# Loading q and k in 1 KB runs of four tokens, with a new order of work around the transposes, in a fused attention and feed-forward kernel

## The chip, the cores and the metric

The kernel runs on one core of a Trainium2 chip. The metric is the device time of one execution in microseconds (us), and lower is better. A run of one program was repeated several times. The engines are PE (matrix multiplications and transposes), VectorE (DVE in the profile), ScalarE (ACT), GpSimd (POOL) and SyncE (SP), which here only issues DMA transfers.

## The reference

The reference computes forgetting attention (causal attention with a decay per token) for 8 batches, 8 heads, 576 tokens and a head size of 64. The result goes straight into a feed-forward block with SiLU.

```python
scores = (q @ k.transpose(0, 1, 3, 2)) / sqrt(D)              # [8, 8, 576, 576]
cum    = cumsum(log(clip(f, 1e-4, 1)), axis=-1)
scores = where(causal, -1e9, scores + cum[..., :, None] - cum[..., None, :])
attn   = softmax(scores)                                      # max, exp, divide by the sum
x      = (attn @ v) -> tokens x (heads * D)                   # [4608, 512]
h      = x @ w_in                                             # [4608, 2048]
out    = (h * sigmoid(h)) @ w_out                             # [4608, 512]
```

q and k are random numbers times 0.1, so the scaled scores are small, and the weights of the attention come mostly from the decay.

## The kernel before

The attention is worked off in 32 pairs of heads (8 batches of 4 pairs). The loop runs once for each pair, `n` from 0 to 31. q and k must be transposed so that the head size lies on the partitions. PE does this by a matrix multiplication with the identity, into PSUM, and VectorE copies the result to SBUF as `qkT`. The scores are then made in three chunks, ScalarE takes the exponential, and VectorE masks the diagonal blocks. For each two pairs PE also makes the denominators (`den`), VectorE takes their reciprocal, and eight DMA transfers spread it over partitions (`rb`). The numerators (`num`) are multiplied by `rb` into `xT`, the input of the feed-forward block.

`fill(n)` puts n pieces of feed-forward work (each four matmuls of 512 columns) between these steps, so that PE has something to do while it waits for the others. There is none before the first 512 tokens of `xT` are complete, which needs a whole batch. So there is a *head*, in which attention runs alone, and a *steady part*, in which PE is nearly always busy.

Each engine works off its instructions in the order in which the program gives them: in the trace of the kernel before, a copy on VectorE whose input was ready at about 228.5 us starts at 231.25, behind a reciprocal of 3.75 us that stands before it in the program. Scores, transposes, denominators and numerators share two PSUM buffers (`psc`).

```python
    psc = ctx.enter_context(tc.tile_pool(name="psc", bufs=2, space=bass.MemoryType.PSUM))
    # ... (cut)
    def load_qk(b, c, h0, h1):                      # issued by GpSimd, converts to bf16
        # ... (cut)
        for i, src in enumerate((q, k)):
            nc.gpsimd.dma_start(
                out=qkb[b][:n, i, c, h0 * D : h1 * D].rearrange("p (h d) -> p h d", d=D),
                in_=src[b, h0:h1, c * P : c * P + n, :].rearrange("h p d -> p h d"),
            )
    # ... (cut)
    def transposes(n):
        # ... (cut)
        tp = psc.tile([P, 2, 1024], BF16, name="tp", tag="sc")
        for i in range(2):                          # q, k
            for c in range(NM + 1):                 # four blocks of 128 tokens, one of 64
                nk = P if c < NM else ST
                nc.tensor.transpose(
                    tp[:, i, c * P : c * P + nk],
                    src[:nk, i, c, p * P : (p + 1) * P],
                    ident_bf[:nk, :nk],
                )
        t = qktp.tile([P, 2, S], BF16, name="qkT", tag="qkT")
        nc.vector.tensor_copy(out=t[:, :, :], in_=tp[:, :, 0:S])      # one copy of 1152 columns
        qkT[n] = t
    # ... (cut)
    def den(qd):                                    # for the pairs 2*qd and 2*qd+1
        # ... 36 small matmuls into dn (cut)
        rec = recp.tile([P, S], FP32, name="rec", tag="rec")
        nc.vector.reciprocal(out=rec[:, :], in_=dn[:, 0:S])
        # ... eight nc.sync.dma_start: rb <- rec (cut)
    # ... (cut)
    for hh in range(2):
        for c in range(NM + 1):
            convert_v(0, c, hh * H // 2, (hh + 1) * H // 2, nc.vector)   # v times its decay
    transposes(0)
    for n in range(NU):
        b, p = divmod(n, NP)
        scores(n, 0)
        fill(1)
        # ... loads of the next batch; convert_v of the next batch on GpSimd (cut)
        scores(n, 1)
        fill(1)
        scores(n, 2)
        fill(2)
        if n % 2 == 0 and n >= 2:
            den(n // 2 - 1)
            fill(2)
        if n % 2 == 1 and n >= 3:
            num(n - 3)
            fill(1)
            num(n - 2)
            fill(1)
            finished(n - 2)
        if n + 1 < NU:
            transposes(n + 1)
        fill(2)
```

The softmax here doesn't subtract the row's maximum and nothing guards it: scores larger than these inputs give would overflow.

## Time and profile before

The time before was 456.11 us (median of 3 runs, 455.33 to 456.65).

The profile is of one execution. Its page gives the busy time of each engine first. Then it divides the span into 40 slices of 11.4 us, and each digit is the busy share in tenths (9 is 90% or more). These are lines of the page of the kernel before:

```profile
span 454.3 us, 7436 instructions
PE 381.1 (84%) x2966; PEld 175.3 (39%) x3013; DVE 232.7 (51%) x337; ACT 202.4 (45%) x312; POOL 118.5 (26%) x154
...
PE   0155236989998999899989998999899989999996
...
DMA  9999999996359635953597309830203021300011
...
DMA packets 128561, 42.57 MB, mean 94 GB/s; under 512 B 115664, under 2 KB 119760, under 8 KB 128528
```

PE is nearly full from the eighth slice on (80 us), and half empty before it. The DMA engines are busy 90% or more in the first nine slices. Most packets are short: one token of one head is 256 bytes.

The view of groups of instructions shows a line of the program, engine, operation, output and input with their sizes, then "busy us, mean ns of one", then the idle time before these instructions and what ended it. The copy of q and k and the two larger masks, before:

```profile
L202 DVE COPY qkT<-tp 128x1152 bf16<-128x1152 bf16 x32 | 23.7, 740 | 16.4 <-PE tp L196 16.4
L253 DVE TENSOR_TENSOR u<-u,mask 128x768 bf16<-128x768 bf16 x32 | 18.4, 575 | 67.8 <-ACT u L240 67.7
L257 DVE TENSOR_TENSOR u<-u,mask 128x256 bf16<-128x256 bf16 x32 | 9.1, 284 | 0.0
```

The view of waits says for which releaser an engine stood still: us in total, number of times, longest. For PE between 167.3 and 303.8 us (three periods of four pairs), before, the largest is:

```profile
PE sc L233 <- DVE qkT L202: 6.9, 6, 1.7
```

The scores wait for the copy of q and k every second pair. The timeline shows why. Its columns are the start and the duration in us, the engine, the line, the operation, and in brackets how long the engine had been idle and what released it. Before, in the steady part:

```profile
226.44 3.75 DVE L293 RECIPROCAL rec<-dn 128x576 f32<-128x576 f32 x1
...
227.55 0.98 PE L196 MATMUL tp<-ident_bf,qkb 128*128 128x128 bf16 x10
...
231.25 0.75 DVE L202 COPY qkT<-tp 128x1152 bf16<-128x1152 bf16 x1
...
232.06 0.39 PE L233 MATMUL sc<-qkT 64*128 64x512 bf16 x2 [1.70 <-DVE qkT L202]
```

The transposes are done soon after 228.5, but their copy stands behind the 3.75 us reciprocal in VectorE's queue. In the head there is another wait, much longer. These are lines of the timeline of the kernel before, around 48 to 62 us:

```profile
48.52 11.05 SPq L299 DMA_DIRECT2D rb<-rec  x8
...
60.86 0.76 DVE L326 TENSOR_TENSOR xT<-nm,rb 128x576 bf16<-128x576 f32 x1 [13.81 <-DMA rb<-rec]
...
61.67 1.46 PE L196 MATMUL tp<-ident_bf,qkb 128*128 128x128 bf16 x10 [13.10 <-DVE xT L326]
```

The reciprocal had ended at 42.0 us. Its broadcasts stood behind the loads of v in the queue of SyncE and were issued from 48.5 to 59.6. PE had no buffer in the meantime.

### The profile page before, as it was taken

What the parts mean: (1) busy time and instruction counts of PE and PEld (TensorE: products, weight loads), DVE (VectorE), ACT (ScalarE), POOL (GpSimd) and SP (SyncE); (2) the same over time, 40 slices, a digit from 0 to 9 for tenths busy, and PEclk for the clock granted to TensorE, in tenths of its full rate; (3) what the DMA queues carried; (4) which work ended last, traced back from release to release, by engine and by line L of the source; (5) the groups of instructions that cost most, each with busy time, mean ns of one, the idle gap of its engine ahead of it and who ended that gap; (6) DMA issues with size and microseconds to landing.
All of it is one profiled execution on the core that took longest, in us unless ns stands there. A gap on an engine that the chain in (4) does not pass through costs nothing.

```text
span 454.3 us, 7436 instructions
## 1 busy us (share of the span) xinstructions
PE 381.1 (84%) x2966; PEld 175.3 (39%) x3013; DVE 232.7 (51%) x337; ACT 202.4 (45%) x312; POOL 118.5 (26%) x154
## 2 busy tenths in 40 slices
PE   0155236989998999899989998999899989999996
PEld 0133113434443444344434443444344434444442
DVE  2335026684468446835683558455845585274310
ACT  3054022564366436643664356435643562264421
POOL 9843943470047004700470047000000000000000
PEclk9999999999999999999999999999999999999999
DMA  9999999996359635953597309830203021300011
GB/s 158 103 180 157 194 184 169 177 115 67 95 133 120 60 100 127 124 57 100 128 116 65 100 25 107 73 100 26 52 25 91 34 52 38 108 1 24 26 68 69
DMA packets 128561, 42.57 MB, mean 94 GB/s; under 512 B 115664, under 2 KB 119760, under 8 KB 128528
## 3 DMA queue, kind: packets, MB, share of 16 engines
q0 software_dynamic: 79392, 13.64, 41.1%
q1 hardware_dynamic: 49136, 28.47, 25.7%
q8 instruction: 23, 0.38, 0.4%
q14 instruction: 10, 0.08, 0.1%
HBM read 36.85 MB, written 9.44 MB: 102 GB/s over the span
## 4 chain that ended last, share of the span: by engine, by line
PE 48%; DMA 13%; issue 12%; DVE 11%; ACT 7%; SPq 4%; POOL 4%; DVEq 0%; POOLq 0%; ACTq 0%
PE po L371 27%; PE hp L344 10%; DMA rb<-rec 8%; ACT u L240 6%; DVE gt L353 5%; PE nm L314 4%; DMA qkb<-in_q_dram 4%; SPq L299 4%; PE sc L233 3%; DVE rec L293 3%; POOL qkb L70 3%; PE tp L196 3%; PE dn L285 1%; DMA qkb<-in_k_dram 1%; ACT th L352 1%
## 5 line engine op out<-in xcount | busy, mean ns | idle before, releaser
L240 ACT ACTIVATE u<-sc 128x1024 bf16<-128x1024 f32 x96 | 97.5, 1028 | 93.9 <-PE sc L233 69.2
L344 PE MATMUL hp<-xT,w_in_bf 128*128 128x512 bf16 x551 | 136.8, 380 | 2.9 <-issue 1.1
L371 PE MATMUL po<-w_out_bf,gt 128*128 128x512 bf16 x554 | 134.3, 380 | 2.6 <-issue 2.1
L353 DVE SCALAR_TENSOR_TENSOR gt<-th,hp 128x512 bf16<-128x512 bf16 x144 | 95.9, 683 | 52.2 <-ACT th L352 52.2
L352 ACT ACTIVATE th<-hp 128x512 bf16<-128x512 f32 x144 | 86.8, 605 | 77.0 <-PE hp L344 70.5
L371 PEld LDWEIGHTS <-gt 128*128 128x128 bf16 x576 | 50.8, 98 | 59.0 <-issue 5.2
L344 PEld LDWEIGHTS <-w_in_bf 128*128 128x128 bf16 x576 | 49.9, 98 | 58.9 <-issue 7.5
L233 PE MATMUL sc<-qkT 64*128 64x512 bf16 (+4 forms) x320 | 40.6, 325 | 31.9 <-DVE qkT L202 26.9
L293 DVE RECIPROCAL rec<-dn 128x576 f32<-128x576 f32 x16 | 60.1, 3755 | 6.3 <-PE dn L285 6.3
L380 ACT ACTIVATE osb<-po 128x512 f32<-128x512 f32 x36 | 21.5, 597 | 73.5 <-PE po L371 46.6
L253 DVE TENSOR_TENSOR u<-u,mask 128x768 bf16<-128x768 bf16 x32 | 18.4, 575 | 67.8 <-ACT u L240 67.7
L70 POOL DMA_DIRECT2D qkb<-in_q_dram x45 | 38.8, 861 | 39.1 <-PE tp L196 34.0
L326 DVE TENSOR_TENSOR xT<-nm,rb 128x576 bf16<-128x576 f32 x32 | 24.2, 756 | 45.0 <-DMA rb<-rec 23.9
L196 PE MATMUL tp<-ident_bf,qkb 128*128 128x128 bf16 (+1 forms) x320 | 34.5, 231 | 13.3 <-DVE xT L326 13.1
L70 POOL DMA_DIRECT2D qkb<-in_k_dram x45 | 38.2, 849 | 11.2 <-DMA w_in_bf<-in_moe_w_in_dram 4.8
L233 PEld LDWEIGHTS <-qkT 64*128 64x128 bf16 x320 | 11.7, 98 | 70.8 <-DVE qkT L202 36.6
L196 PEld LDWEIGHTS <-qkb 128*128 128x128 bf16 (+1 forms) x320 | 24.3, 102 | 28.8 <-issue 15.4
L202 DVE COPY qkT<-tp 128x1152 bf16<-128x1152 bf16 x32 | 23.7, 740 | 16.4 <-PE tp L196 16.4
L314 PE MATMUL nm<-u,vp 128*64 128x64 bf16 (+4 forms) x512 | 30.0, 264 | 0.2
L314 PEld LDWEIGHTS <-vp 128*64 128x64 bf16 x512 | 20.1, 117 | 17.9 <-issue 12.7
L155 PE MATMUL wps<-ident_f,wexp 64*128 64x64 f32 x5 | 0.8, 322 | 17.8 <-POOL ident_f masks.py:199 17.8
L285 PEld LDWEIGHTS <-w_bf 128*32 128x32 bf16 (+1 forms) x576 | 10.9, 100 | 10.8 <-issue 6.4
(73 smaller groups left out, 121.0 us busy)
## 6 DMA issues: line engine op xcount, KB each, us to landing
rb<-rec SPq DMA_DIRECT2D x128, 72.0 KB, 2.1
out_dram<-osb SPq DMA_DIRECT2D x36, 256.0 KB, 2.0
qkb<-in_q_dram POOLq DMA_DIRECT2D x28, 128.0 KB, 6.8
qkb<-in_k_dram POOLq DMA_DIRECT2D x28, 128.0 KB, 7.0
w_in_bf<-in_moe_w_in_dram POOLq DMA_DIRECT2D x4, 512.0 KB, 10.0
w_out_bf<-in_moe_w_out_dram POOLq DMA_DIRECT2D x4, 512.0 KB, 11.4
qkb<-in_q_dram POOLq DMA_DIRECT2D x15, 64.0 KB, 5.9
qkb<-in_k_dram POOLq DMA_DIRECT2D x15, 64.0 KB, 5.8
```

The costliest lines, as they stand in the source:

```text
L70: nc.gpsimd.dma_start(out=qkb[b][:n, i, c, h0 * D : h1 * D].rearrange("p (h d) -> p h d", d=D), in_=src[b, h0:h1, c * P : c * P + n, :].re ...
L196: nc.tensor.transpose(tp[:, i, c * P : c * P + nk], src[:nk, i, c, p * P : (p + 1) * P], ident_bf[:nk, :nk],)
L202: nc.vector.tensor_copy(out=t[:, :, :], in_=tp[:, :, 0:S])
L233: nc.tensor.matmul(sc[:, i, col : col + q1 - q0], lhsT=t[r, 1, kb * P : (kb + 1) * P], rhs=t[r, 0, q0:q1], start=True, stop=True,)
L240: nc.scalar.activation(out=u[:, :, c * 512 : (c + 1) * 512], in_=sc[:, :, :], func=ACT.Exp, scale=scale)
L293: nc.vector.reciprocal(out=rec[:, :], in_=dn[:, 0:S])
L314: nc.tensor.matmul(nm[i * D : (i + 1) * D, q0:q1], lhsT=v_t[r, p, :] if kb == NM else vp[:, kb, 2 * p + i, :], rhs=(ut[r, :] if kb == NM e ...
L326: nc.vector.tensor_tensor(out=xT[:, p, b * S : (b + 1) * S], in0=nm[:, 0:S], in1=rb[:, :], op=ALU.mult)
L344: nc.tensor.matmul(hp[:, :], lhsT=w_in_bf[:, cc, fc * P : (fc + 1) * P], rhs=xT[:, cc, t0 : t0 + TG], start=(cc == 0), stop=(cc == NCC - 1),)
L352: nc.scalar.activation(out=th[:, :], in_=hp[:, :], func=ACT.Tanh, scale=0.5)
L353: nc.vector.scalar_tensor_tensor(out=gt[:, fc, :], in0=th[:, :], scalar=1.0, in1=hp[:, :], op0=ALU.add, op1=ALU.mult,)
L371: nc.tensor.matmul(po[:, :], lhsT=gt[:, fc, tb * P : (tb + 1) * P], rhs=w_out_bf[:, fc, :], start=(fc == 0), stop=(fc == NFC - 1),)
```

## The change

The intent: shorten the head, and free the copy of q and k from the reciprocal.

1. *Loads.* q and k are loaded by SyncE as fp32, one pair at a time, with four tokens in a row on one partition. One piece is then 4 x 256 bytes = 1 KB instead of 256 bytes. GpSimd converts them to bf16. The last 64 tokens of a batch are loaded apart.
2. *Order of tokens.* Partition p now holds the tokens 4p to 4p+3. After the transposes the columns in PSUM are in the order (j, p) instead of (p, j), so VectorE reorders when it copies. One copy becomes three.
3. *Order of work.* The transposes of the next pair come ahead of the denominators. The reciprocal is done in two halves, with fill work between. The numerators of two pairs come one iteration earlier.
4. *Along with it.* v of batch 0 is now multiplied by its decay on GpSimd, not on VectorE before the first pair. It stands in the program at the third pair, but GpSimd runs ahead and comes to it sooner (at 17.46 us in the trace after, where the third pair starts at 35.4). The weights are loaded later (`w_in` at n = 2, `w_out` at n = 6).

The diff, cut to its core:

```diff
-    def load_qk(b, c, h0, h1):
+    def load_qk(n):
+        b, p = divmod(n, NP)
         ...
+            nc.sync.dma_start(
+                out=t[:, :, :],
+                in_=src[b, 2 * p : 2 * p + 2, 0:SM, :].rearrange("h (p j) d -> p h (j d)", j=NJ),
+            )
         ...  (load_tails, cast_qk, cast_tails: cut)
     def transposes(n):
         ...
+            for j in range(NJ):
                 nc.tensor.transpose(
+                    tp[:, i, j * P : (j + 1) * P], src[:, i, j, :], ident_bf[:, :]
                 )
         ...
-        nc.vector.tensor_copy(out=t[:, :, :], in_=tp[:, :, 0:S])
+        for i in range(2):
+            nc.vector.tensor_copy(
+                out=t[:, i, 0:SM].rearrange("r (p j) -> r j p", j=NJ),
+                in_=tp[:, i, 0:SM].rearrange("r (j p) -> r j p", j=NJ),
+            )
+        nc.vector.tensor_copy(out=t[:, :, SM:S], in_=tp[:, :, SM:S])
         ...
+    def rec_part(qd, part):
+        dn, rec = dens[qd]
+        r = slice(part * S // 2, (part + 1) * S // 2)
+        nc.vector.reciprocal(out=rec[:, r], in_=dn[:, r])
         ...
     for n in range(NU):
         b, p = divmod(n, NP)
         scores(n, 0)
         fill(1)
+        if n + 1 < NU:
+            last_cast = cast_qk(n + 1, (nc.gpsimd, nc.gpsimd))
+        if n + 4 < NU:
+            load_qk(n + 4)
+        if n == 2:
+            with tc.issue_after(last_cast.ins):
+                for c in range(NM + 1):
+                    convert_v(0, c, 0, H, nc.gpsimd)
+                for i in range(WQ):
+                    load_w_in(i)
+        if n == 6:
+            with tc.issue_after(last_cast.ins):
+                for i in range(WQ):
+                    load_w_out(i)
         ...
         scores(n, 2)
         fill(2)
-        if n % 2 == 0 and n >= 2:
-            den(n // 2 - 1)
-            fill(2)
-        if n % 2 == 1 and n >= 3:
-            num(n - 3)
+        if n + 1 < NU:
+            transposes(n + 1)
+        fill(1)
+        if n % 2 == 1:
             fill(1)
+            den(n // 2)
+            rec_part(n // 2, 0)
+            fill(1)
+            rec_part(n // 2, 1)
+            fill(1)
+        elif n >= 2:
             num(n - 2)
             fill(1)
-            finished(n - 2)
-        if n + 1 < NU:
-            transposes(n + 1)
-        fill(2)
-    den(NU // 2 - 1)
+            num(n - 1)
+            fill(2)
+            finished(n - 1)
```

## The prediction

> **What bounds the kernel now.** Two regimes. From 80 us on, the tensor engine (PE) binds: in the windows view it is busy 94 to 95% (37.3 of 40 us at 160-200, 95.3 of 100 at 300-400), and in the chain of waits the same place of the loop returns every 45.1 to 46.1 us per four head pairs, 11.4 us a pair. Before 80 us PE works only about 30 us. The first feed-forward matmul of a ready group comes near 81 us.
>
> The head's causes, in the timeline: GpSimd issues 20 q/k loads of 0.75 to 0.85 us each until 16.7 us, and only then builds the identities, so the first transposes start at 18.5 and the first scores at 24.0. The DMA engines are saturated (page: nine tenths for the first 8 slices; 115664 of 128561 packets under 512 B). The copy of the next q/k stands behind the 3.76 us reciprocal (PE idle 3.1 us at 39.5). The reciprocal's broadcast DMAs stand behind value loads on the sync queue: they are issued from 48.5 to 59.6 although the reciprocal ended at 42.0, and PE is idle from 48.6 to 61.7.
>
> **Removed.** The q/k loads on GpSimd (77 us of its queue). About 73,700 short q/k packets become some 24,600, of which 16,400 are 1 KB[...]. Head: scores start at about 12 us (estimate: decay weights ready at 8.0 as now, transposes 0.8 + 1.5, copies 1.5), not 24. Transposes ahead of the denominators free the copy from the reciprocal: in steady state that wait costs PE 1.7 + 0.9 us per four pairs. Numerators of a pair of pairs come one iteration earlier, so group 0 is ready at the start of n=5, not at the end.
>
> **Added.** Copy out of PSUM: one of 740 ns becomes three. [...] +24 us of VectorE in all (51% to some 60%), off the path in steady state, about +0.7 us a pair in the head. GpSimd gets casts of perhaps 0.6 to 1 us each (estimate from its 1.04 us for a 128x512 multiply), 2 a pair: hidden. More loads go through the sync queue, so broadcasts may still wait. PE work itself doesn't change.
>
> **Sum.** Estimated head: pairs 0 and 1 at 5.7 us, 2 to 4 at 8 to 11 us because reciprocal and broadcast still hold the two PSUM buffers. Iteration 5 starts, with feed-forward work to fill in, at about 55 us. Before, iteration 6 starts near 83.5; one pair of 11.4 us apart, so the head gains about 17 us. 27 iterations at 11.1 us (were 11.35; floor 10.8) give 300, the end (one leftover run of fills, numerators, 64 chunks at 0.865, last store) about 70: 55 + 300 + 70 = 425. Predicted 426 us, range 413 to 442; faster by over 2%: 0.92, within 2%: 0.05, slower: 0.03.
>
> **What would show it.** Right: timeline with scores by 13 us, feed-forward by 60; PE in the windows at 0-80 up from 30 to about 50 us; q/k copies near 1.5 us per pair; under 85,000 packets; the steady waits of scores for the copy gone; period of four pairs at 44 to 45 us. Wrong: period over 45.5 us, with PE waiting for VectorE (gt, rec) instead.
>
> **What would make it wrong.** Broadcasts stuck behind q/k and value loads on the one sync queue; weights, now issued only after pair 3's casts, arriving after 55 us; denominators, now right behind their own scores, waiting for masks; GpSimd casts slowing VectorE.

With the other go the three terms of the copies, which came to 1.5 us a pair. The rest counts with it: +24 us of VectorE is 32 x (1.5 - 0.74), and the +0.7 us a pair in the head is the same difference. The sum came to 55 + 300 + 70 = 425 us, put down as 426.

## The result, and the profile after

The time after was 448.81 us (median of 4 runs, 448.28 to 450.13). The ratio is 0.984, with a 95% interval of 0.981 to 0.987: 1.6% faster. That is clear of the noise, but under 2%. Ratios in this document are the mean time of one kernel's fast runs over that of the kernel before's fast runs of the same rounds. They are not quite the ratios of the medians quoted. The prediction, 426 us, asked for four times that gain, and the measured time lies outside its range.

The same lines of the page after (slices of 11.2 us):

```profile
span 448.4 us, 7690 instructions
PE 390.3 (87%) x3013; PEld 177.7 (40%) x3013; DVE 290.5 (65%) x406; ACT 204.7 (46%) x312; POOL 97.5 (22%) x149
...
PE   2236676899979999999989998999899989999996
...
DMA  8995959975666365425642423250203020400011
...
DMA packets 79156, 52.03 MB, mean 116 GB/s; under 512 B 49872, under 2 KB 70352, under 8 KB 79120
```

The loads did what was asked of them. There are 79,156 packets instead of 128,561, and PE works earlier. VectorE is the surprise: 290.5 us busy instead of 232.7. The groups after show from where:

```profile
L243 DVE COPY qkT<-tp 128x512 bf16<-128x512 bf16 x64 | 79.2, 1322 | 27.4 <-PE tp L238 27.4
L247 DVE COPY qkT<-tp 128x128 bf16<-128x128 bf16 x32 | 8.1, 252 | 0.0
L298 DVE TENSOR_TENSOR u<-u,mask 128x768 bf16<-128x768 bf16 x32 | 22.2, 692 | 32.1 <-ACT u L285 32.1
L302 DVE TENSOR_TENSOR u<-u,mask 128x256 bf16<-128x256 bf16 x32 | 12.9, 402 | 0.0
```

The copies of one pair take 1.32 + 1.32 + 0.25 = 2.9 us, where one took 0.74. The prediction had 1.5. The masks, which nobody touched, are longer on average as well: 692 instead of 575 ns and 402 instead of 284 ns.

The waits of PE in the same window (167.3 to 303.8 us), after:

```profile
PE hp L396 <- DVE gt L405: 3.0, 3, 1.0
PE sc L278 <- ACT u L285: 1.8, 6, 0.3
```

The wait of the scores for the copy has gone, as intended. In its place PE waits for the SiLU product `gt` on VectorE. The timeline after shows how that comes about:

```profile
217.27 2.45 DVE L243 COPY qkT<-tp 128x512 bf16<-128x512 bf16 x2
...
219.65 1.25 DVE L405 SCALAR_TENSOR_TENSOR gt<-th,hp 128x512 bf16<-128x512 bf16 x2
...
223.23 1.94 DVE L343 RECIPROCAL rec<-dn 128x288 f32<-128x288 f32 x1
...
225.77 1.02 PE L396 MATMUL hp<-xT,w_in_bf 128*128 128x512 bf16 x4 [0.99 <-DVE gt L405]
```

From 217.27 to 225.8 VectorE has no gap in this stretch. The copies push the `gt` and the two halves of the reciprocal back, and at the end PE has no free buffer for its next feed-forward chunk.

In the head, two places stand out. The first is at 17 to 24 us, in the timeline after:

```profile
17.46 1.04 POOL L210 TENSOR_TENSOR vp<-vf_118,w_bf 128x512 bf16<-128x512 f32 x1
17.50 1.41 DVE L298 TENSOR_TENSOR u<-u,mask 128x768 bf16<-128x768 bf16 x1
...
18.84 3.21 DVE L302 TENSOR_TENSOR u<-u,mask 128x256 bf16<-128x256 bf16 x1
19.40 1.05 POOL L210 TENSOR_TENSOR vp<-vf_119,w_bf 128x512 bf16<-128x512 f32 x1
20.40 1.04 POOL L210 TENSOR_TENSOR vp<-vf_120,w_bf 128x512 bf16<-128x512 f32 x1
...
24.57 0.98 PE L278 MATMUL sc<-qkT 64*128 64x512 bf16 x4 [8.21 <-DVE qkT L247]
...
29.81 3.96 DVE L298 TENSOR_TENSOR u<-u,mask 128x768 bf16<-128x768 bf16 x1
30.32 1.03 POOL L210 TENSOR_TENSOR vp<-vf_215,w_bf 128x512 bf16<-128x512 f32 x1
...
32.33 1.03 POOL L210 TENSOR_TENSOR vp<-vf_217,w_bf 128x512 bf16<-128x512 f32 x1
```

A mask of 128x256 that takes 0.28 us elsewhere takes 3.21 us while GpSimd multiplies v (and, between the multiplications, issues loads of weights). The copy of k waits behind it, and PE waits 8.2 us. In the next pair a mask of 128x768, 0.56 us elsewhere, takes 3.96 us: it ends only after three multiplications in a row (30.32 to 33.36). What is not wrong in this head are the first broadcasts of the reciprocal, which stood behind the loads of v in the kernel before. Here they are issued as soon as the reciprocal has ended:

```profile
35.52 3.77 DVE L343 RECIPROCAL rec<-dn 128x288 f32<-128x288 f32 x2 [0.16 <-PE dn L331]
...
39.31 5.02 SPq L351 DMA_DIRECT2D rb<-rec  x8
```

The second place is at 60 to 71 us:

```profile
61.06 3.03 POOL L164 DMA_DIRECT2D w_out_bf<-in_moe_w_out_dram  x4
...
70.28 0.76 DVE L378 TENSOR_TENSOR xT<-nm,rb 128x576 bf16<-128x576 f32 x1 [6.40 <-DMA rb<-rec]
71.10 0.58 PE L396 MATMUL hp<-xT,w_in_bf 128*128 128x512 bf16 x1 [4.15 <-DVE xT L378]
```

The broadcast of the reciprocal lands late (up to 7.6 us after issue instead of a median of 2.0) while the output weights are being loaded.

### The profile page after: what moved, and what is told of

The parts are those of the page before. It is cut to its first block, busy times and chain, and to the rows that moved or that the text cites. A ratio compares the mean times of both kernels' runs of the same rounds, so it can differ in the third digit from the quotient of the medians.

```text
span 448.4 us, 7690 instructions
## 1 busy us (share of the span) xinstructions
PE 390.3 (87%) x3013; PEld 177.7 (40%) x3013; DVE 290.5 (65%) x406; ACT 204.7 (46%) x312; POOL 97.5 (22%) x149
## 2 busy tenths in 40 slices
DMA packets 79156, 52.03 MB, mean 116 GB/s; under 512 B 49872, under 2 KB 70352, under 8 KB 79120
## 4 chain that ended last, share of the span: by engine, by line
PE 54%; DVE 25%; ACT 11%; issue 5%; DMA 3%; SPq 1%; POOL 0%; DVEq 0%; ACTq 0%; POOLq 0%
PE po L423 28%; PE hp L396 11%; ACT u L285 7%; DVE qkT L243 7%; DVE gt L405 6%; DVE rec L343 6%; PE nm L366 5%; PE sc L278 3%; DVE u L298 3%; PE tp L235 3%; PE dn L331 2%; DMA rb<-rec 2%; ACT osb L432 2%; ACT th L404 2%; DVE u L302 1%
## 5 line engine op out<-in xcount | busy, mean ns | idle before, releaser
L396 PE MATMUL hp<-xT,w_in_bf 128*128 128x512 bf16 x576 | 141.7, 385 | 12.2 <-DVE gt L405 6.8
L423 PE MATMUL po<-w_out_bf,gt 128*128 128x512 bf16 x576 | 137.9, 380 | 0.0
L243 DVE COPY qkT<-tp 128x512 bf16<-128x512 bf16 x64 | 79.2, 1322 | 27.4 <-PE tp L238 27.4
L396 PEld LDWEIGHTS <-w_in_bf 128*128 128x128 bf16 x576 | 50.9, 98 | 67.4 <-issue 16.5
L343 DVE RECIPROCAL rec<-dn 128x288 f32<-128x288 f32 x32 | 61.2, 1936 | 4.5 <-PE dn L331 4.5
L95 POOL CAST qkb<-qf 128x512 bf16<-128x512 f32 x31 | 19.1, 615 | 197.3 <-issue 114.9
L298 DVE TENSOR_TENSOR u<-u,mask 128x768 bf16<-128x768 bf16 x32 | 22.2, 692 | 32.1 <-ACT u L285 32.1
L278 PEld LDWEIGHTS <-qkT 64*128 64x128 bf16 x320 | 13.5, 97 | 66.3 <-issue 51.2
L366 PEld LDWEIGHTS <-vp 128*64 128x64 bf16 x512 | 19.5, 117 | 22.6 <-DVE qkT L247 10.6
L235 PE MATMUL tp<-ident_bf,qkb 128*128 128x128 bf16 x256 | 27.6, 236 | 0.7 <-ACT u L285 0.5
L235 PEld LDWEIGHTS <-qkb 128*128 128x128 bf16 x256 | 18.2, 104 | 8.6 <-issue 0.5
L95 POOL CAST qkb<-kf 128x512 bf16<-128x512 f32 x32 | 20.6, 643 | 3.0 <-DMA kf<-in_k_dram 3.0
L331 PE MATMUL dn<-u,w_bf 128*32 128x64 bf16 (+4 forms) x512 | 16.0, 261 | 5.9 <-DVE u L298 5.9
L331 PEld LDWEIGHTS <-w_bf 128*32 128x32 bf16 (+1 forms) x576 | 11.3, 99 | 17.1 <-issue 13.1
## 6 DMA issues: line engine op xcount, KB each, us to landing
w_out_bf<-in_moe_w_out_dram POOLq DMA_DIRECT2D x4, 512.0 KB, 11.2
```

The lines of the kernel that those rows point to most:

```text
L95: ins = engs[i].tensor_copy(out=t2[:, i, :, :].rearrange("p j (h d) -> p h j d", d=D), in_=t[:, :, :].rearrange("p h (j d) -> p h j d", d=D),)
L235: nc.tensor.transpose(tp[:, i, j * P : (j + 1) * P], src[:, i, j, :], ident_bf[:, :])
L243: nc.vector.tensor_copy(out=t[:, i, 0:SM].rearrange("r (p j) -> r j p", j=NJ), in_=tp[:, i, 0:SM].rearrange("r (j p) -> r j p", j=NJ),)
L278: nc.tensor.matmul(sc[:, i, col : col + q1 - q0], lhsT=t[r, 1, kb * P : (kb + 1) * P], rhs=t[r, 0, q0:q1], start=True, stop=True,)
L331: nc.tensor.matmul(dn[32 * j : 32 * j + 32, q0:q1], lhsT=w_bf[r, kb, bh : bh + 1].to_broadcast([nk, 32]), rhs=rhs, start=(kb == 0), stop=( ...
L343: nc.vector.reciprocal(out=rec[:, r], in_=dn[:, r])
```

## The experiments

To place a gain or a loss, the text uses two numbers of each profiled run: when the first scores matmul of pair 7 starts in the timeline, and the mean time per pair from there to pair 31 (24 pairs). Pair 7 at a later time means a longer head. In the new order the rest from the start of pair 31 is always 77.6 to 78.2 us. In the old order it is 85.5 us (86.5 in e2), since more is left over, so the pair 7 of an old order must not be set against the pair 7 of a new one without those 8 us.

| kernel | median us | ratio to before | pair 7 starts | us per pair |
|---|---|---|---|---|
| before | 456.11 | 1 | 95.9 (old order) | 11.37 |
| after | 448.81 | 0.984 | 95.8 | 11.46 |
| e1_order_alone | 450.44 | 0.986 | 106.2 | 11.03 |
| e2_loads_alone | 495.33 | 1.084 | 96.1 (old order) | 12.98 |
| e3_plain_copy | 433.86 | 0.949 | 88.5 | 11.08 |
| e4_v01_vector | 445.17 | 0.975 | 91.4 | 11.46 |
| e6_strided_read | 438.19 | 0.958 | 91.4 | 11.15 |
| e9_k_on_scalar | 452.13 | 0.989 | 91.0 | 11.73 |
| e11_matmul_reorder | 446.26 | 0.976 | 89.7 | 11.54 |
| e7_wout_n3 | 451.92 (451.21 without a slow run) | 0.985, unclear | 93.3 | 11.46 |
| e12_read_v01 | 437.61 | 0.958 | 91.6 | 11.15 |
| e13_read_v01_vpool | 440.99 | 0.966 | 95.5 | 11.14 |
| e14_read_late_v1 | 433.09 | 0.949 | 85.5 | 11.16 |
| e15_late_v1_wout_n4 | 433.51 | 0.950 | 86.3 | 11.18 |

Theories, rivals to each other as to where the predicted 30 us went:

- *The copy*: the reordering copy is so dear that VectorE holds PE up.
- *The values*: GpSimd's multiplications of v hold up VectorE's masks. A rival inside it: the casts of q and k on GpSimd do.
- *The transfers*: broadcasts and loads share a queue or the DMA engines, and the broadcasts come late in the head. The loads of the output weights at pair 6 are one form of it.
- *The order*: the new order of work was not worth what was predicted.

The texts call some of these theories by letters, or by their part of the change. In the later runs, E is the theory of the output weights. F is the theory that the broadcasts stand behind the loads of v in one queue, and G its rival, that the shared DMA engines and not the queue delay them.

### e1_order_alone: the new order with the old loads

The kernel before, with only the new end of the loop and the divided reciprocal:

```diff
 (kernel before)
+        if n + 1 < NU:
+            transposes(n + 1)
+        fill(1)
+        if n % 2 == 1:
+            ... den(n // 2), rec_part in halves, as in the change
+        elif n >= 2:
+            ... num(n - 2), num(n - 1), as in the change
```

> The kernel before with only the new order (transposes ahead of denominators and numerators, denominators one iteration earlier, reciprocal in two halves); loads and the single 0.74 us copy as before. Theory A (the slow copies of 2.9 us a pair ate the steady gain of the new order): the period of four pairs falls from 45.5 to about 44 us, PE waits for the copy are gone, and no wait for gt comes in its place; the head still starts at 24 us, and feed-forward work comes one iteration earlier; total 435 to 445 us. Rival B (the new order is worth nothing in steady state, since denominators now wait for their own masks): period stays 45.3 to 45.7, total 448 to 455.

Measured: 450.44 us, ratio 0.986 (0.982 to 0.989). In the steady part a pair takes 11.03 us, and a period of four pairs 44.1 us, always. The waits for the copy are gone: in the window from 167.3 to 303.8 us PE waits only for ScalarE, 1.8 us in six pieces. So the order is worth what was predicted (11.1 per pair), with a copy of 0.75 us. The total missed the 435 to 445 us expected, because pair 4 took 23.1 us: PE waits 14.5 us there for broadcasts that stand behind the loads of v (the reciprocal ended at 62.0, they were issued from 72.5).

The step from e1 to the change is the addition of the new loads and what they entail. Pair 7 comes 10.4 us sooner (106.2 to 95.8), and each of 24 pairs takes 0.43 us longer (11.03 to 11.46), 10.2 us in all. That is how a large change moved the time little: the loads gave 10 us in the head and took it back in the steady part. One reserve on the clock: the view of windows gives 0.94 for the first 80 us of e1 and 1.00 for the change. These figures are not safe for the heads. The same view gives 1.00 for 71.0 to 76.5 us of the change, where four feed-forward matmuls in a row take 1.89 us instead of 1.04. The first scores of pair 2 take 0.61 us in both heads (0.39 in the steady part), so no difference of clock shows between them.

### e2_loads_alone: the new loads with the old order

```diff
 (kernel after)
-        ... the new end of the loop, rec_part in halves
+        ... the end of the loop and the undivided reciprocal of the kernel before
```

> The changed kernel with the old order of transposes, denominators and numerators and an undivided reciprocal. The copy (2.9 us) again stands behind the reciprocal (3.76 us). Theory A: the wait of scores for the copy grows by 2.1 us where it existed, so the period is 47 us or more; the head gains its 12 us at the start but loses to slow masks; total 452 to 462 us. Rival B (order worth nothing): period about 45.5, total within 3 us of the changed kernel, 446 to 452.

Measured: 495.33 us, ratio 1.084 (1.080 to 1.088). The direction was expected, the size was not. A 2.9 us copy behind everything else in the iteration, with only two fill chunks (1.9 us) to cover it, stops the scores of every pair. The timeline of this run holds the rest of the explanation:

```profile
199.41 0.39 PE L278 MATMUL sc<-qkT 64*128 64x512 bf16 x2 [3.24 <-DVE qkT L247]
...
201.47 1.89 PE L390 MATMUL hp<-xT,w_in_bf 128*128 128x512 bf16 x4
```

After the idle 3.24 us, four feed-forward matmuls take 1.89 us, where they take 1.02 to 1.04 us elsewhere (the ends of matmuls are modelled in the profile). The view of windows gives a granted clock of 0.63 for 199.4 to 204.0 us. After the shorter waits of the same run, 1.10 us at 213.4 and 1.67 us at 225.5, they take 1.04, and the view gives 1.00 for 226.0 to 230.6 us. So here the wait of 3.24 us cost more than itself. How much of the 495 is this and how much is waiting was not taken apart.

### e3_plain_copy: the copy of before, with a wrong order of tokens

It copies as the kernel before did, and leaves the tokens of q and k in the wrong order. Its output is wrong, which doesn't matter for the time. (The comparison with the reference still passed, since the scores are so small. So for all kernels here that reorder differently, the order was made sure of from the access patterns, not from that comparison.)

```diff
-        for i in range(2):
-            nc.vector.tensor_copy(... reordering ...)
-        nc.vector.tensor_copy(out=t[:, :, SM:S], in_=tp[:, :, SM:S])
+        nc.vector.tensor_copy(out=t[:, :, :], in_=tp[:, :, 0:S])
```

> WRONG RESULT ON PURPOSE: the changed kernel with the three reordering copies put back to one contiguous copy of 1152 columns (about 0.74 us), so tokens stay in the wrong order; all else equal. It measures what the reordering itself costs. Theory A: VectorE loses 68 us of busy time, the wait of PE for gt goes, period 44 us, head shorter by about 2 us a pair; total 430 to 438 us. Rival B (copies are hidden off the path): total 445 to 449.

Measured: 433.86 us, ratio 0.949 (0.945 to 0.953). A pair takes 11.08 us, and pair 7 starts at 88.5. The copying alone is worth 15 us of the missing 23. In the profiled runs, whose spans differ by 16.4 us, 24 x 0.375 = 9.0 us of it (11.455 less 11.08 per pair) lie in the steady part and 7.3 us before pair 7.

### e4_v01_vector: v of the first two batches multiplied on VectorE

```diff
-                    convert_v(0, c, 0, H, nc.gpsimd)
+                    convert_v(0, c, 0, H, nc.vector)
 ...
-                    convert_v(b + 1, c, 0, H, nc.gpsimd)
+                    convert_v(b + 1, c, 0, H, nc.gpsimd if b else nc.vector)
```

> The changed kernel with the value multiplies of batches 0 and 1 on VectorE instead of GpSimd; those of later batches stay. Theory C (in the head the masks, two SBUF inputs, are stretched from 0.56 and 0.28 to as much as 4 us while GpSimd runs a two-input multiply): masks of pairs 0 and 1 return to 0.56, 0.28, 0.18 us, the scores of pair 2 begin 5 to 8 us earlier than 35.4, VectorE gets 9 us of multiplies more; total 441 to 446 us. Rival D (masks are stretched by something else, the casts or DMA writes): masks stay stretched, total 448 to 452.

Measured: 445.17 us, ratio 0.975 (0.971 to 0.979), 3.6 us less than the change. The masks of the first pair, in the timeline of this run:

```profile
15.54 0.56 DVE L298 TENSOR_TENSOR u<-u,mask 128x768 bf16<-128x768 bf16 x1 [1.19 <-ACT u L285]
16.01 0.73 DVE L302 TENSOR_TENSOR u<-u,mask 128x256 bf16<-128x256 bf16 x1
16.66 0.59 DVE L305 TENSOR_TENSOR ut<-ut,mask_t 128x64 bf16<-128x64 bf16 x1
```

They were 1.41, 3.21 and 1.35 us. What is left of the stretch, 0.73 instead of 0.28 and 0.59 instead of 0.18, is next to GpSimd's casts (15.99 to 17.22 us), which are still there and which no run took away. So the multiplications of v were the main cause. In the trace of the change the mask did not end between two GpSimd multiplications: the mask at 29.81 lasted 3.96 us instead of 0.56, to 33.77, and three multiplications in a row were over at 33.36. Why they hold each other up is not shown. The 3.21 us mask is less clear. No multiplication shows during its first 0.5 us, only the issue of a load of weights, and no run took these issues away.

Pair 2 started at 27.9 instead of 35.4, 7.5 us sooner. At pair 7 only 4.4 us of this were left. The rest was lost at pair 2, which took 13.8 us instead of 10.6: its broadcasts were issued from 36.8, though the reciprocal had ended at 32.1. In the change they were not late. This delay comes up only once pairs 0 and 1 are quick, and e12 to e14 look into it.

### e6_strided_read: the same reordering with the stride on the other side

The reordering copy reads PSUM in order and writes SBUF with a step of four elements (2-byte pieces, 8 bytes apart). It can as well write in order and read with a step. The mapping of elements is the same.

```diff
-                out=t[:, i, 0:SM].rearrange("r (p j) -> r j p", j=NJ),
-                in_=tp[:, i, 0:SM].rearrange("r (j p) -> r j p", j=NJ),
+                out=t[:, i, 0:SM].rearrange("r (p j) -> r p j", j=NJ),
+                in_=tp[:, i, 0:SM].rearrange("r (j p) -> r p j", j=NJ),
```

> The changed kernel with the two reordering copies turned round: the write to SBUF runs in order, the read from PSUM steps by 128 columns (same result). What makes the copy cost 1.2 to 1.3 us instead of the 0.65 predicted? If it is the write (2-byte pieces 8 bytes apart), this copy takes 0.6 to 0.7 us[...], the wait for gt goes, the period is 44.1 to 44.4 us, total 436 to 441. If any step other than 1 costs that much on either side, it stays at 1.2 to 1.3 us and the total at 447 to 450.

Measured: 438.19 us, ratio 0.958 (0.953 to 0.963), 10.6 us less than the change. The group of this run:

```profile
L243 DVE COPY qkT<-tp 128x512 bf16<-128x512 bf16 x64 | 41.6, 685 | 26.7 <-PE tp L238 26.7
```

So 0.685 us instead of 1.322, for the same elements. The author had estimated 0.65, which is near the strided read; the strided *write* takes 1.9 times as long. An estimate of the time per element: the kernel before copies 1152 elements in 740 ns and e6 128 elements in 214 ns, both in order, so about 0.51 ns for one element and 150 ns fixed. With the same fixed part the strided read costs (685 - 150) / 512 = 1.04 ns and the strided write 2.29 ns. So in these copies the stride cost time on either side, and more on the write.

Steady part: 11.15 us per pair, 7.3 us less in 24 pairs, and the waits of PE in the window from 167.3 to 303.8 us no longer list `gt`. Head: 4.4 us less at pair 7. Within it, pairs 0 and 1 took 7.5 and 6.9 us instead of 12.3 and 10.8. That is more than the copies save (2 x 1.3), because the masks now ran ahead of most of the multiplications of v: they took 0.90, 1.12 and 0.18 us, although GpSimd still did those. So the two losses, copy and masks, were partly one: in the profile of the change the long copy had pushed the masks under the multiplications (e7 shows that this was a close race).

### e9_k_on_scalar: the copy of k on ScalarE

Rival: VectorE's queue is too full, and another engine should do half.

```diff
-                nc.vector.tensor_copy(out=o, in_=s)          # both
+                q: nc.vector.tensor_copy(out=o, in_=s)
+                k: nc.scalar.activation(out=o, in_=s, func=ACT.Copy)
```

> The changed kernel with the k half of the reordering copy on ScalarE, q half and tail on VectorE, strided write as before. Theory A (VectorE full): 1.2 us a pair leave VectorE, its wait for PE to gt shrinks, period about 44.3; ScalarE, at 46%, takes the copy in about 0.6 us if it pays nothing for the strided write, over 1.2 if it does; total 438 to 444. If instead ScalarE's extra work delays the exps: period 45.5 or more, total 448 or more.

Measured: 452.13 us, ratio 0.989 (0.984 to 0.993). The group of ScalarE in this run:

```profile
L248 ACT ACTIVATE qkT<-tp 128x512 bf16<-128x512 bf16 x32 | 42.2, 1318 | 37.5 <-DVE qkT L246 37.5
```

ScalarE takes 1318 ns for the same write, where VectorE took 1322. It looks like a cost of the write itself, not of VectorE; ScalarE with the other direction was not tried. Pair 7 starts 4.8 us sooner (its first masks took 0.57, 1.12 and 0.18 us, see e7), but a pair takes 11.73 us. From 170 to 300 us VectorE's copy of the tail waits 13.4 us in all, in 12 pieces, for ScalarE's copy, and PE waits 1.3 us in each period for the reciprocal, which comes later on VectorE.

### e11_matmul_reorder: PE writes PSUM in order of tokens

Another place for the stride: PE itself writes the transposed block with a step. This run uses an ordinary matmul with the identity and fp32 in PSUM; no run here has a transpose of bf16 with that step. The tail goes into a buffer of its own.

```diff
-                nc.tensor.transpose(
-                    tp[:, i, j * P : (j + 1) * P], src[:, i, j, :], ident_bf[:, :]
-                )
+                nc.tensor.matmul(
+                    tp[:, i, :].rearrange("r (p j) -> r j p", j=NJ)[:, j, :],
+                    lhsT=src[:, i, j, :],
+                    rhs=ident_bf[:, :],
+                    start=True, stop=True,
+                )
 ...
+        nc.vector.tensor_copy(out=t[:, :, 0:SM], in_=tp[:, :, :])
+        nc.vector.tensor_copy(out=t[:, :, SM:S], in_=tq[:, :, :])
```

> The changed kernel with the reordering given to PE: plain matmuls by the identity write fp32 into PSUM with a step of four columns[...], then one contiguous copy of 1024 fp32 columns and one of 128. Same result. Theory A: copies 1.2 + 0.25 us a pair instead of 2.9, VectorE loses 45 us of busy time, PE time for these 10 matmuls stays near 0.9 us a pair if a stepped PSUM write is free; period 44.1 to 44.4, total 437 to 442. If the stepped write slows PE: matmuls of 128 columns well over 0.1 us each, period 45 or more.

Measured: 446.26 us, ratio 0.976 (0.971 to 0.980). VectorE is relieved (1.22 + 0.28 us per pair), but PE pays:

```profile
L236 PE MATMUL tp<-ident_bf,qkb 128*128 128x128 bf16 x256 | 43.8, 337 | 1.1 <-ACT u L290 1.0
```

The mean of these matmuls was 236 ns in e6 and is 337 here (medians of 219 and 314 between 170 and 300 us). The shortest pair of the period grew from 10.29 to 10.71 us, and PE is the bottleneck there. The run changed the step, the type and the kind of instruction together, though, so the share of the step alone is not shown.

### e7_wout_n3: the output weights loaded three pairs sooner

```diff
-        if n == 6:
+        if n == 3:
             with tc.issue_after(last_cast.ins):
                 for i in range(WQ):
                     load_w_out(i)
```

> The changed kernel with the four output-weight loads issued at pair 3 instead of pair 6. Theory E (the 7.6 us landing of the reciprocal broadcast, and so PE's stop from 66.9 to 71.1, comes from the weight loads issued at 61 to 64 us sharing the DMA engines): broadcast lands in about 2 us, pair 5 takes 12 to 13 us instead of 17.6, total 443 to 445. Rival F (the value loads on the same queue are the cause): broadcast still lands in 5 us or more, total 447 to 450.

Measured: 451.92 us as a median of all four runs, 447.59 to 454.45, one of them slow (451.21 without it), ratio 0.985 (0.978 to 0.992), unclear. In the profiled run, the fastest, the broadcasts of the reciprocal around pair 5 landed in 2.0 to 2.2 us, and pair 5 took 12.4 us instead of 17.6: the weights were the cause there. But pair 2 took 18.2 us, because a broadcast was now late at that place (VectorE waits 8.4 us for `rb`). The delay moved and the time did not improve.

The comparison with the 10.6 us of the change is not clean, since pair 2 started at 27.9 here and at 35.4 there. Pairs 0 and 1 took 8.2 and 7.4 us, although nothing before pair 3 was edited. The traces show a race: GpSimd's first multiplication and the first mask begin at 17.46 and 17.50 us in the change, and at 17.47 and 17.51 here. In the change the multiplication took 1.04 us and the mask 1.41; here the mask took 0.57 and the multiplication 1.51, and the masks after it 1.12 and 0.18 instead of 3.21 and 1.35. Two patterns turn up in the profiles: e2 has the masks of the change to a hundredth (1.41, 3.21, 1.35), and e9 and e11, which also leave these multiplications on GpSimd, have those of e7. Whether single executions of one kernel differ in this too is not shown, so the three runs of the change that were not profiled may have lost less there.

### e12_read_v01: e4 and e6 together

```diff
 (e6_strided_read)
-                    convert_v(0, c, 0, H, nc.gpsimd)
+                    convert_v(0, c, 0, H, nc.vector)
 ... and batch 1 likewise, as in e4
```

> The changed kernel with the in-order write of the copy (as the strided-read run, 438 us) and the value multiplies of batches 0 and 1 on VectorE. If the two costs are separate: the head loses a further 2 to 4 us, total 434 to 437. If the stretched masks only hid the next wait (broadcasts of the reciprocal behind batch 1's value loads on the sync queue), the scores of pair 3 begin at 41 to 43 us as in both single runs, total 437 to 439.

Measured: 437.61 us, ratio 0.958 (0.956 to 0.961). If the gains added, it would have been about 434.5 (438.19 - 3.6). Pair 7 starts at 91.6, as in e6 and in e4. The timeline of this run shows what held it:

```profile
35.51 0.69 DVE L210 TENSOR_TENSOR vp<-vf,w_bf 128x512 bf16<-128x512 f32 x1 [6.73 <-DMA vf<-in_v_dram]
...
38.14 5.02 SPq L351 DMA_DIRECT2D rb<-rec  x8
...
38.96 1.49 PE L366 MATMUL nm<-u,vp 128*64 128x512 bf16 x16 [6.80 <-DVE qkT L247]
```

VectorE runs its queue in order. The multiplications of batch 1's values, now in that queue, wait 6.7 us for a load that took 17.45 us to land, and everything behind them waits too, the copy of q and k among it. The reciprocal had been done at 28.8, but its broadcasts were issued from 38.1: on SyncE they stand behind those same loads.

### e13_read_v01_vpool: the loads of v issued by GpSimd

```diff
 (e12_read_v01)
-            nc.sync.dma_start(out=vst[b][c]..., in_=v[...])
+            nc.gpsimd.dma_start(out=vst[b][c]..., in_=v[...])
```

> As the run before it in this call, but value loads are issued by GpSimd, so they no longer stand in front of the broadcasts on the sync queue. Theory F (queue order): the first broadcast is issued within 1 us of the end of the reciprocal, pair 2 takes 9 to 11 us instead of 17, total 428 to 433. Rival G (the shared DMA engines, not the queue, are the limit): broadcasts are issued early but land 5 us or more later, total 434 to 438.

Measured: 440.99 us, ratio 0.966 (0.963 to 0.969), worse than e12. The queue theory is half right. With the values out of SyncE's queue the broadcasts were issued at 37.02, at once when the reciprocal ended, at 37.0. But they landed slowly (a median of 5.6 us over the first 100 us), as the rival G expected. And the first scores started at 16.4 instead of 11.0: the tail of k landed 10.88 us after its issue at 3.23 us (4.1 at most in the first 20 us of the change), now that GpSimd issued the loads of v, and PE waited 4.7 us for the cast of a tail. The total is above what either theory expected. Pair 7 starts at 95.5.

### e14_read_late_v1: the values of batch 1 loaded later

If the trouble at pair 2 is that batch 1's values are asked for much too soon, then they can be asked for later, which frees the queue and the DMA engines. This kernel has the in-order write of e6 and batch 0's values on VectorE as e4. It loads batch 1's values at pair 2 instead of pair 0, and multiplies them on VectorE at pair 4. Later batches are as in the change.

```diff
 (e6_strided_read)
-                    convert_v(0, c, 0, H, nc.gpsimd)
+                    convert_v(0, c, 0, H, nc.vector)
 ...
             if p == 0:
                 load_tails(b + 1)
-                for c in range(NM + 1):
-                    load_v(b + 1, c, 0, H)
-            if p == 2:
+                if b == 1:
+                    for c in range(NM + 1):
+                        convert_v(1, c, 0, H, nc.vector)
+                if b > 0:
+                    for c in range(NM + 1):
+                        load_v(b + 1, c, 0, H)
+            if p == 2 and b == 0:
+                cast_tails(1)
+                for c in range(NM + 1):
+                    load_v(1, c, 0, H)
+            elif p == 2:
                 cast_tails(b + 1)
                 for c in range(2):
                     convert_v(b + 1, c, 0, H, nc.gpsimd)
-            if p == 3:
+            if p == 3 and b > 0:
```

> As the first run of this call, but batch 1's value loads are given to the sync queue only at pair 2, behind the first broadcasts, and multiplied at pair 4. Both theories F and G expect the first broadcast issued at once, landing in 2 to 3 us, since fewer loads are in flight: pair 2 takes 9 to 12 us, total 428 to 434. If values then come too late for pair 4's numerators at pair 6, the time is lost again there: total 436 or more.

Measured: 433.09 us (432.73 to 433.42), ratio 0.949 (0.946 to 0.951). It is the fastest kernel here that is right: about 3.5% below the change and 5.1% below the kernel before. In its timeline:

```profile
29.32 6.06 SPq L351 DMA_DIRECT2D rb<-rec  x8
...
37.39 0.61 PE L278 MATMUL sc<-qkT 64*128 64x512 bf16 x2 [3.37 <-DVE xT L378]
```

The reciprocal ended at 29.3 and its broadcasts were issued at 29.3. Pair 2 took 12.2 us (25.2 to 37.4) instead of 18.1 in e12. Pair 7 starts at 85.5, 6.1 us sooner than in e12, and the steady part is that of e6. The gain over e12, 4.5 us, is a little less than that. Two waits of e12 went together here, that of the broadcasts and that of VectorE for the values. In e6 VectorE does not wait for values, the broadcasts are late all the same (the reciprocal ends at 29.3, they are issued from 34.7), and pair 3 starts at 43.0 as in e12. So the broadcasts alone were enough to hold it.

### e15_late_v1_wout_n4: e14 with the output weights at pair 4

```diff
 (e14_read_late_v1)
-        if n == 6:
+        if n == 4:
```

> As the 433 us version (in-order write of the copy, value multiplies of batches 0 and 1 on VectorE, batch 1's values loaded at pair 2), with the output-weight loads at pair 4 instead of 6, between the first two sets of broadcasts. Theory E (weight loads make the second set of broadcasts land late, pair 5 takes 16.5 us): pair 5 takes 12 to 13 us, total 429 to 432. If the loads only move the delay to pair 3 or 4, as pair 2 took it over in the earlier run with early output weights: total 432 to 436.

Measured: 433.51 us, ratio 0.950 (0.948 to 0.951), the same as e14. Pair 5 took 11.2 us instead of 16.5, but pair 3 took 12.8 instead of 7.8, and pair 2 13.5 instead of 12.2. The output weights delayed the pairs on which they fell. Moving them gave nothing in two tries (e7 and e15). Which resource they share with the broadcasts (the DMA engines, or the order within them) was not settled. One reserve here too: the view gives the profiled run of e14 a granted clock of 0.81 in the first 80 us and that of e15 1.00. The first scores of pairs 2 to 5 take 0.61 us in both, and the other runs of e14 had mean clocks of 1.00 over their spans and took the same time, so the clock does not explain the total, but single pairs of the two heads should not be compared to a tenth.

## Why the prediction was wrong

The prediction was 55 us to the start of pair 5, 27 pairs of 11.1 us, and 70 us for the rest. Measured after the change: pair 5 starts at 64.95 (10 us later), the 27 pairs take 317.5 us (17.5 more), and the rest takes 66 (4 less).

- **"Scores start at about 12 us", fewer packets: right.** The first scores start at 12.27 us, not 23.99. There are 79,156 packets, below the 85,000 named. Loads of q and k land in a median of 3.1 and 3.3 us instead of 6.8 and 7.0, with pieces of twice the size. Which part the longer packets have in this is not shown: the loads also left GpSimd, which now builds the identities from 0.75 us on, and not at 16.7 behind its loads, and no run takes the two apart.
- **The steady waits of the scores for the copy gone: right.** They have gone, and e1 shows that the order alone brings a pair to 11.03 us, where the prediction had 11.1.
- **"q/k copies near 1.5 us per pair": the step that failed.** The estimate behind it was not shown by any trace, and with the strided write the copies took 1.32 + 1.32 + 0.25 = 2.9 us. With the stride on the read they took 0.685 + 0.685 + 0.21 = 1.6 us (e6), almost the estimate. VectorE went to 65%, not to "some 60%".
- **"Off the path in steady state": wrong with it.** With copies of 2.9 us, VectorE was without a gap around each reciprocal, and PE waited for `gt`: 0.99 us in each period. The period is 45.5 us, not 44 to 45. This is the sign that the prediction named for being wrong, though the settled period of 45.48 us stays just under the 45.5 named with it. e3 and e6 show that with a cheaper copy the period is 44.1 to 44.3. The mechanism foretold was right, and the size of one term undid it. In the steady part this is 7.3 of the 11.8 us by which the profiled span of e6 is shorter than that of the change.
- **"Pairs 0 and 1 at 5.7 us": the step that failed in the head.** They took 12.3 and 10.8 us, 11.7 us more in all. "GpSimd gets casts ... hidden" overlooked what else GpSimd got. The casts were nearly hidden. But the change also moved the multiplications of v for batch 0 to GpSimd, beside the first masks. The prediction did not cost that, and named "GpSimd casts slowing VectorE" only as a risk. The masks took up to 3.21 us beside these, and up to 3.96 us beside those of batch 1 (e4 removes both). Together with the longer copy this held pair 2 to 35.4 us, where e12, without both, has 24.9.
- **"Pairs 2 to 4 at 8 to 11 us": right, but by luck.** They took 10.6, 8.2 and 10.7 us, so pair 5, at 65 and not at "about 55 us", is late by what pairs 0 and 1 lost. The broadcasts' place behind the loads of v was named among the things that could make the prediction wrong, and left out of the sum. It cost nothing here: the first two sets were issued at 39.31 and 58.19, as the reciprocals ended. But with quick pairs 0 and 1 they are late, and pair 2 takes 17.6 us (e6) and 18.1 (e12). So the sum would have been wrong there too. With this mended, and the two points above, pair 5 starts at 55.9, and the whole takes 433 (e14).
- **Pair 5, and the weights.** The prediction counted every pair from 5 on at 11.1 us. Pair 5 took 17.6 and pair 6 13.3, 8.6 us more than that. The output weights fall on pair 5. Moving them removed this wait and made another (e7, e15), and left pair 6 as it was (13.3 and 13.1).
- **"PE in the windows at 0-80 up from 30 to about 50 us": wrong.** It rose from 30.4 to 40.7. In e14 it is 48.4.

So of the 22.8 us between 426 and 448.8, the copy and the values with their loads account for 15.7 (e14 does both: 433.1). The remaining 7 us are about as long as the surplus of pair 5 and pair 6; e15 shows that it is not to be had by moving the weights, and what is behind it stays open.

## What to carry to other kernels

When a copy from PSUM to SBUF has to reorder 2-byte elements, try the stride on the read and write in order: this was the same two lines here, and worth 10.6 us. When a change moves work to an idle engine, look up what else it touches at that moment, because it can cost more than the work moved: here a mask of 0.28 us took 3.21 beside GpSimd's multiplications, and broadcasts stood 9 us behind loads in one queue (e12). And where a change gives in one stage, test the stages apart: set against e1, a head that was 10 us shorter and a steady part that was 10 us longer looked like a change without effect.
